# A wider look-ahead window in the build-time plan of TensorE's work

## The chip, the cores and the metric

The kernel runs on one core of a Trainium2 chip. The metric is the device time of one execution in microseconds, taken as the median of several runs. TensorE (PE) multiplies matrices, VectorE (DVE), ScalarE (ACT) and GpSimd (POOL) do the elementwise work, and SyncE (SP) issues most DMAs. Each engine works through its own queue in order; between engines, semaphores order the work. Matrix products land in eight PSUM banks of 512 fp32 columns.

## The reference

One transformer block on 2048 tokens of width 1024, in bf16:

```
h   = x + attention(layernorm(x))
out = h + ((relu(n W_gate) * (n W_up)) W_down),   n = layernorm(h),  W_gate, W_up: 1024 x 3584

attention(n):
  q, k, v = split(n W_qkv) into 32 heads of 32
  pq, pk  = phi(q), phi(k)          # phi(t) = (t + 1 if t > 0 else exp(t)) + 1e-6
  kv, z   = pk^T v, sum over tokens of pk
  o       = (pq kv) / (pq z + 1e-6)
  return o W_o
```

## The kernel before

All large products are done by a seven-product form of the 2 x 2 block matrix product (Strassen-Winograd). A `Quad` holds one such block: its methods `p1` to `p7` issue the seven products, each into a PSUM bank; `fork` copies a bank to a second bank and `snap` copies one to SBUF, both on ScalarE; `out` holds what is done with a finished quarter. Products 1, 6 and 7 add onto one bank (A), 5 and 3 onto another (E); product 2 adds onto the copy of A, product 4 onto A itself. `Quads.run` interleaves quads: products 4 and 3 of a quad are issued after product 1 of the next. Sums and differences of the operand blocks are made beforehand by VectorE.

The stages, in order of time: the first layernorm with K and V (to about 120 us), Q and the attention output (about 120 to 220 us), gate and up (220 to 569 us), and down, where each of the seven products is itself a seven-product block (`deep`, 569 us to the end).

The stage around the first part of the change is the second. Each of the 16 token tiles (`Tile_`) has numerator products (`group` 0, 1 and 2: three, three and two matmuls of 132 columns), divided by the denominators on ScalarE and VectorE into `o`; a transposing DMA into `oT`; and the output projection `wo` in two halves of eight 512-column matmuls. `group` and `wo` take turns with PSUM banks 5, 6 and 7. VectorE adds the input to each half of `wo` and so empties its bank; from this come `h`, its normalisation (one pass on ScalarE, one on POOL), a second transposing DMA, and the operand sums `left_sums`. The function `steps` lays out numerators of tile m beside `wo` of tile m - 2. Into this list the quads of Q for the second half of the tokens (`q_quad(1, c, ...)`) put their products of four matmuls.

In the gate and up stage, `load_group` loads weight columns, `GW.sums` makes their differences on VectorE, `wd_sums` loads a row of W_down, makes four differences and stores them to DRAM (`r_dram`), and `spill` stores sums of the activations (`s_dram`, `l_dram`).

None of this is issued as it is written. From line 568 to the end of `block_kernel`, `nc` is a `Plan`, which records every call as a node with what it must wait for; consecutive matmuls onto one bank that form one accumulation are one node. `Plan.issue` then sorts all nodes by a model of the machine (`cost`, `schedule`) and issues them in that order, with each engine's order fixed. Every instruction therefore has line 123 in the profile.

For TensorE, each node has a nominal time `nom`: the sum of the durations of the matmuls written before it. When TensorE is free, `schedule` takes, of the nodes that are ready, the one with the lowest `nom`, but it looks only at nodes within `WINDOW` nanoseconds of the oldest node that is not yet placed:

```
limit = nodes[pe[first]].nom + self.WINDOW
a = [i for i in a if nodes[i].nom <= limit]
```

The other engines go by `late`, the latest time at which a node may start. Nodes on one engine are taken to follow each other with no delay (`r = clock[e] if w.eng == e else end`), two DMAs on SP too.

Of the kernel before, what the change touches and what calls it, by code (L numbers as in the profile page):

```python
# [32 lines left out]
class Plan:  # L33
# [3 lines left out]

    G = 64
    SEM = 100.0
    WINDOW = 6000.0  # L40
    AHEAD = 120000.0
    OPENING = 45000.0
    MIXED = (120000.0, 215000.0)
# [159 lines left out]
    def schedule(self):  # L203
# [14 lines left out]
        while True:  # L218
            best = None
            for e in engines:  # L220
# [8 lines left out]
                if e == "tensor":  # L229
                    while first < len(pe) and pe[first] in done:  # L230
                        first += 1
                    limit = nodes[pe[first]].nom + self.WINDOW
                    a = [i for i in a if nodes[i].nom <= limit]
# [1340 lines left out]
```

## Time and profile before

| | us |
|---|---|
| median of 7 runs | 724.74 (724.42 to 725.39) |
| profiled execution | 725.2 |
| its span | 723.4 |
| TensorE busy | 711.4 (98%) |
| VectorE busy | 568.9 (79%) |
| ScalarE busy | 278.0 (38%) |
| POOL busy | 56.5 (8%) |

The span is the time from the first to the last instruction of the profiled execution; 1.8 us lie around it. Times in the text are microseconds from the start of the span. The trace is of one execution, the median that of seven runs, and the two differ by 0.5 us. "PE" in a row is a matmul, "PEld" a weight load; a name before the arrow is written, one after it read (`mem` is the one SBUF tile, `psum` the PSUM tile, `tiny` the small one). In the list of waits, a row has the waiting engine, what it waited for, and total, count and longest wait.

### The profile page before, as it was taken

The numbers are of one execution on the slowest core, as the hardware profiler recorded it, in microseconds if no ns is written. First come the engines' busy times: TensorE is split into PE (matmuls) and PEld (weight loads), VectorE is DVE, ScalarE is ACT, GpSimd is POOL, SyncE is SP. The second block draws the span as 40 slices with busy tenths as digits, with TensorE's granted clock in tenths as the row PEclk, the third lists the DMA queues.
The fourth block names the chain that finished last, engine by engine and source line by source line (L and its number), as shares of the span: only waits on it lengthen the run. The fifth ranks groups of instructions, "written<-read, shape, count | busy, mean of one in ns | idle before, by whom it ended". The sixth has DMA issues, their size and how long they took to land.

```text
span 723.4 us, 11146 instructions
## 1 busy us (share of the span) xinstructions
PE 711.4 (98%) x4112; PEld 396.8 (55%) x4163; DVE 568.9 (79%) x966; ACT 278.0 (38%) x548; POOL 56.5 (8%) x62
## 2 busy tenths in 40 slices
PE   8899999999999999999999999999999999999998
PEld 4444445444444444444444444444444688888887
DVE  6899665788797975666766968769768879899996
ACT  5787655665655343333333333333333220001100
POOL 0000000002101120000000000000000004001452
PEclk9999999999999999999999999999999999999999
DMA  9556506159955540446245584685591878777974
GB/s 290 147 97 134 163 1 200 35 109 199 213 107 146 137 96 8 134 129 189 64 138 178 170 258 132 205 261 182 165 299 57 277 266 206 217 263 241 244 76 60
DMA packets 156503, 117.40 MB, mean 162 GB/s; under 512 B 54944, under 2 KB 140192, under 8 KB 156320
## 3 DMA queue, kind: packets, MB, share of 16 engines
q1 hardware_dynamic: 148832, 113.01, 53.8%
q0 software_dynamic: 7616, 3.67, 4.8%
q8 instruction: 32, 0.52, 0.3%
q14 instruction: 23, 0.19, 0.1%
HBM read 70.52 MB, written 34.08 MB: 145 GB/s over the span
## 4 chain that ended last, share of the span: by engine, by line
PE 87%; DVE 6%; DMA 3%; ACT 3%; issue 1%; SPq 0%; DVEq 0%; ACTq 0%
PE psum L123 87%; DVE mem L123 5%; ACT mem L123 2%; DMA mem<-mem 2%; DMA mem<-in_A_wqkv_dram 1%; DVE tiny L123 1%; ACT tiny L123 1%; SPq L123 0%; ACT psum L123 0%; DVEq L123 0%; ACTq L123 0%
## 5 line engine op out<-in xcount | busy, mean ns | idle before, releaser
L123 PE MATMUL psum<-mem 128*128 128x512 bf16 (+4 forms) x4096 | 710.6, 334 | 8.6 <-DVE mem L123 2.6
L123 PEld LDWEIGHTS <-mem 128*128 128x128 f16 (+1 forms) x4163 | 396.8, 98 | 322.9 <-issue 9.5
L123 DVE TENSOR_TENSOR mem<-psum,mem 128x512 f32<-128x512 f32 (+2 forms) x240 | 187.2, 793 | 97.4 <-ACT mem L123 64.7
L123 DVE TENSOR_TENSOR mem<-mem 128x512 f16<-128x512 bf16 (+8 forms) x400 | 241.1, 643 | 9.7 <-DMA mem<-mem 3.7
L123 ACT COPY mem<-psum 128x512 f32<-128x512 f32 (+2 forms) x124 | 92.6, 749 | 212.4 <-PE psum L123 206.2
L123 ACT COPY psum<-psum 128x512 f32<-128x512 f32 (+1 forms) x68 | 49.1, 722 | 157.9 <-PE psum L123 157.9
L123 POOL DMA_DIRECT2D out_dram<-mem x28 | 34.1, 1300 | 412.1 <-DVE mem L123 412.0
L123 ACT ACTIVATE mem<-psum 128x512 bf16<-128x512 f32 x90 | 53.5, 597 | 19.8 <-PE psum L123 19.2
L123 DVE SCALAR_TENSOR_TENSOR mem<-mem 128x512 bf16<-128x512 bf16 (+1 forms) x71 | 57.6, 812 | 1.2
L123 DVE SCALAR_TENSOR_TENSOR mem<-psum,mem 128x512 bf16<-128x512 f32 x66 | 45.4, 689 | 14.8 <-PE psum L123 12.5
L123 POOL TENSOR_SCALAR mem<-mem,tiny 128x1024 bf16<-128x1024 bf16 x16 | 20.7, 1296 | 244.2 <-ACT tiny L123 244.2
L123 ACT ACTIVATE mem<-mem,tiny 128x1024 bf16<-128x1024 bf16 x24 | 27.5, 1145 | 5.2 <-DVE tiny L123 5.0
L123 DVE TENSOR_SCALAR mem<-mem 128x512 bf16<-128x512 bf16 (+1 forms) x49 | 16.5, 339 | 15.4 <-ACT mem L123 15.1
L123 ACT ACTIVATE tiny<-tiny 128x1 f32<-128x1 f32 (+2 forms) x120 | 23.9, 205 | 7.4 <-DVE tiny L123 4.5
L123 ACT ACTIVATE mem<-mem 128x1024 bf16<-128x1024 f32 (+1 forms) x23 | 24.3, 1056 | 5.1 <-DVE mem L123 3.1
L123 DVE TENSOR_TENSOR mem<-psum,tiny 128x384 bf16<-128x384 f32 (+1 forms) x48 | 22.8, 507 | 4.0 <-ACT tiny L123 3.5
L123 ACT ACTIVATE tiny<-psum 128x12 f32<-128x12 f32 (+1 forms) x48 | 8.0, 170 | 18.5 <-PE psum L123 17.8
L123 DVE BATCH_NORM_STATS2 tiny<-mem 128x6 f32<-128x512 bf16 x16 | 10.3, 680 | 2.3 <-DMA mem<-in_A_x_dram 2.3
L123 ACT CAST mem<-psum 128x512 bf16<-128x512 f32 x18 | 10.3, 581 | 3.3 <-PE psum L123 2.9
L123 DVE TENSOR_SCALAR mem<-mem,tiny 128x1024 bf16<-128x1024 bf16 x16 | 8.6, 540 | 3.7 <-ACT tiny L123 3.6
L123 ACT ACTIVATION_READ_ACCUMULATOR mem<-mem,tiny 128x1 f32 x24 | 4.5, 188 | 0.0
L123 DVE TENSOR_SCALAR tiny<-tiny 128x1 f32<-128x1 f32 x16 | 3.4, 210 | 0.4
(17 smaller groups left out, 12.2 us busy)
## 6 DMA issues: line engine op xcount, KB each, us to landing
l_dram<-mem SPq DMA_DIRECT2D x98, 128.0 KB, 2.3
mem<-l_dram SPq DMA_DIRECT2D x12, 896.0 KB, 6.2
mem<-in_A_x_dram SPq DMA_DIRECT2D x32, 256.0 KB, 3.1
mem<-in_B_W_up_dram SPq DMA_DIRECT2D x14, 512.0 KB, 5.6
mem<-in_B_W_gate_dram SPq DMA_DIRECT2D x14, 512.0 KB, 4.5
mem<-in_B_W_down_dram SPq DMA_DIRECT2D x28, 256.0 KB, 3.5
r_dram<-mem SPq DMA_DIRECT2D x56, 128.0 KB, 2.4
mem<-r_dram SPq DMA_DIRECT2D x8, 896.0 KB, 5.1
```

The costliest lines, as they stand in the source:

```text
L123: call = lambda: getattr(getattr(self.nc, eng), op)(*args, **k)
```

## The change

One constant of the planner changes. The window within which it may pull a TensorE node ahead of older ones grows from 6000 to 10000 ns of nominal matmul time. The number of instructions, their sizes and the memory layout stay; the order on TensorE, VectorE, ScalarE and SP is planned anew.

```
 class Plan:
     G = 64
     SEM = 100.0
-    WINDOW = 6000.0
+    WINDOW = 10000.0
     AHEAD = 120000.0
     OPENING = 45000.0
     MIXED = (120000.0, 215000.0)
...
                 if e == "tensor":
                     while first < len(pe) and pe[first] in done:
                         first += 1
                     limit = nodes[pe[first]].nom + self.WINDOW
                     a = [i for i in a if nodes[i].nom <= limit]
                     if not a:
                         continue
```

More of the change, by code (lines that the diff above doesn't have):

```diff
@@ L39 @@
     SEM = 100.0
-    WINDOW = 6000.0
+    WINDOW = 10000.0
     AHEAD = 120000.0
```

## The prediction

> **What bounds the kernel now.** First the busy shares, then TensorE's clock, then the chain that ended last.
>
> ```profile
> PE 711.4 (98%) x4112; PEld 396.8 (55%) x4163; DVE 568.9 (79%) x966; ACT 278.0 (38%) x548; POOL 56.5 (8%) x62
> ...
> PEclk9999999999999999999999999999999999999999
> ...
> PE 87%; DVE 6%; DMA 3%; ACT 3%; issue 1%; SPq 0%; DVEq 0%; ACTq 0%
> ```
>
> TensorE is busy 98% of the span at the full granted clock and carries 87% of the chain. The change adds or removes no instruction, so it can only fill TensorE's idle time or make more of it. How much is there? Ends of matmuls are modelled, so I use starts: in a full stretch a 512-column matmul starts every 0.2158 us, and 4163 weight loads against 4112 matmul records mean that 51 records are missing; a gap of exactly one matmul is a missing record unless the weight loads (none is missing) show it too. What remains after 140 us is short:
>
> ```
> at us    idle   what TensorE went on with
> 148.66   0.14   numerator products
> 150.76   0.89   output projection (wo) of tile 0
> 165.34   0.21   wo, tile 3, first half
> 170.63   0.51   wo, tile 4, first half
> 175.92   0.51   wo, tile 5, first half
> 193.46   0.16   product 3 of a Q quad
> 206.75   0.39   product 6 of a gate/up quad
> 268.58   0.20   product 3 of a gate/up quad
> 573.81   0.10   product 6 of a down quad
> ```
>
> Together 3.1 us, 0.43% of the time: that is all that this change can win. Nothing stands between 270 and 570 us, nor after 574. TensorE's waits between 148 and 270 us and the stages say the same:
>
> ```profile
> PE psum L123 <- DMA mem<-mem: 0.7, 1, 0.7
> PE psum L123 <- DVE mem L123: 0.7, 2, 0.3
> PE psum L123 <- ACT psum L123: 0.2, 1, 0.2
> ...
> 154.69:182.94 28.25, 27.35 (x151) 13.31 (x151) 22.50 (x54) 17.37 (x59) 6.38 (x6) 1.00 0.90 192
> ...
> 217.30:568.86 351.56, 349.94 (x1625) 160.34 (x1653) 260.12 (x462) 125.99 (x201) 11.19 (x8) 1.00 0.53 157
> ```
>
> The columns of the stage rows are stretch, length, busy PE, PEld, DVE, ACT and POOL, clock, DMA share, GB/s. The chain shows what is behind the largest gaps:
>
> ```profile
> 147.51 3.20 DMA mem<-mem
> 150.71 0.05 issue
> 150.76 2.88 PE psum L123 x14
> ...
> 163.53 0.77 DVE mem L123
> 164.30 0.30 issue
> 164.60 0.18 DVE mem L123
> 164.78 0.43 issue
> 165.21 0.09 DVE mem L123
> 165.29 0.04 issue
> 165.34 1.01 PE psum L123 x4
> ```
>
> The first is the transposing DMA that turns tile 0's attention output for wo. The second is a PSUM bank: the next wo needs the bank of the wo before it, which VectorE empties only after a 1.15 us subtraction that stands ahead in its queue:
>
> ```profile
> 163.53 1.15 DVE L123 TENSOR_TENSOR mem<-mem 128x1024 f16<-128x1024 bf16 x1
> 164.60 0.68 DVE L123 SCALAR_TENSOR_TENSOR mem<-psum,mem 128x512 bf16<-128x512 f32 x1
> ```
>
> The gaps at 170.63 and 175.92 have the same pair ahead of them (1.15 us from 168.81 and from 174.10).
>
> **The change, part by part.** A wider WINDOW lets the planner take a TensorE group whose nominal place lies up to 10 us behind the oldest unplaced group instead of 6 us. Comparing the two instruction orders, TensorE's is the same up to about 150 us; 104 of its 957 groups change places, at 150-183, 192-202, 206-211 and 571-587 us of the present trace. VectorE, ScalarE and SP are reordered there, and VectorE and SP also at about 390-550 us. POOL keeps its order.
>
> *150-183 us.* In steps of six numerator matmuls, one product, wo, two numerators, wo, the products shift by one:
>
> ```
> filler ahead of wo of tile   0    1    2    3    4        5        between wo 6 and wo 7
> before                       -    p6   p5   p7   p2       p1 next  p4
> after                        p6   p5   p7   p2   p1 next  p4       -
> ```
>
> The gap at 150.76 is thus filled. Product 6 has four matmuls, 4 x 0.2158 = 0.863 us; it adds onto a bank whose copy (ScalarE, 148.51 to 149.09) is done, so it runs 149.87 to 150.73 and wo 0 starts at 150.76 as before. The gain comes 32 us later, where no product stands between wo 6 and wo 7: -0.86.
>
> Here the Trainium skill speaks against the change: "TensorE: Matmul & The Clock Gate", under "Back-to-back issue gap", says that a sustained load-and-multiply stream settles at about 131 ns for a 512-column matmul. Product 6 would then be 0.52 us of work: 0.34 us less to win and 0.36 us of the gap left. This trace has 215.8 ns in every full stretch; I take the trace.
>
> The next stalls change because the evacuations come a step earlier. I follow the queues with this trace's durations: last matmul start to its reader 0.41 us (0.25 for a 132-column one), ScalarE to VectorE 0.04, VectorE to TensorE 0.06.
> - Tile 3 (0.21): the 1.15 us subtraction is no longer ahead of the bank read. VectorE reads at 164.10 (bound by wo itself) to 164.78 and TensorE arrives at 165.13: no stall, -0.21.
> - Tile 4 (0.51): the same; bank read 168.89-169.57, TensorE at 169.91: -0.51.
> - Tile 5 (0.51): one subtraction now does stand ahead, 173.14-174.29, then the read to 174.89. TensorE arrives at 174.70 and starts at 174.95: 0.25 is left, -0.26.
> - Wo of tile 7, late next: TensorE arrives 0.97 us closer to the normalisation that precedes its transposing DMA. VectorE ends that at 178.51, TensorE arrives at 181.97. The eight such transposes between 147 and 180 us land 3.04 to 4.18 us after issue, mean 3.30, the one for this tile 3.56. At 3.56 it lands at 182.10: +0.19, between 0 and +0.8.
>
> *192-202 us.* A numerator matmul moves ahead, 0.06 us of fill in the 0.16 us gap; VectorE gets one subtraction of 0.68 us earlier, into the 0.4 us that it waits for ScalarE. I take -0.05, bounds -0.16 to +0.3.
>
> *206-211 us.* Product 6 waits for ScalarE's bank copy (0.57 us); now product 5, whose bank is free, goes first: -0.39. Two numerators then come 0.86 us sooner against a VectorE read, by the same following +0.14.
>
> *571-587 us.* Products of the first two down quads are interleaved otherwise; the copy that product 6 waits for again has one 0.76 us group beside it: 0, bounds -0.1 to +0.8 (one such group uncovered).
>
> *390-550 us, VectorE and SP.* W_down subtractions (0.42 us each) and their DMAs move. They cost nothing while TensorE's products cover them: 12.1 us of matmuls a quad against about 9 us of VectorE (260.12 of 351.56 busy), with 1.8 us to spare in the banks (the product that reuses a bank comes two products of 1.73 us later; the read takes 0.41 + 1.22 of these). Uncovered, each lateness counts in full. On SP one move sets a wait, see the second rival.
>
> Sum: -0.86 -0.21 -0.51 -0.26 +0.19 -0.05 -0.39 +0.14 = -1.95, say **-1.9 us**. The profiled execution took 725.2 us (span 723.4, 1.8 around it), the median of the seven runs is 724.74; what is around the span does not change. 725.2 becomes 723.3, the median **722.8 us**. A difference of 0.2%, 1.45 us, is about what a measurement of this kernel tells from no change, so the forecast is just past it.
>
> **Rivals.**
> 1. *The gain is given back at once.* The first fill only moves TensorE 0.86 us closer to what is late next, and in steps with wo on both sides VectorE's and ScalarE's latencies set the pace (the chain between 160 and 180 us is 25% DVE and 29% ACT and only 32% PE). If tile 7's transpose takes 4.18 us (+0.8 instead of +0.19) and one bank read is late again (+0.5), -0.85 is left: 723.9, no difference that can be told. For it: transposes are slowest at 174 us, where the DMA engines are busy 90%. Against it: each subtraction that made a bank late has visibly moved.
> 2. *Slower: SP blocks.* At 473.6 us the new order puts the load of a W_down row directly behind the stores that read its buffer. SP issues in order, so it stands until the store has landed:
>
> ```profile
> 471.21 2.44 SPq L123 DMA_DIRECT2D r_dram<-mem  x3
> 474.25 0.38 SPq L123 DMA_DIRECT2D mem<-in_B_W_gate_dram  x1
> 474.68 2.14 SPq L123 DMA_DIRECT2D s_dram<-mem  x2
> 476.91 0.41 SPq L123 DMA_DIRECT2D mem<-in_B_W_up_dram  x1
> ```
>
> That store landed at 477.58, 6.4 us after its issue, behind two 512 KB weight loads. So SP stands 3.9 us, and behind it wait two spills and the last group's second gate and up halves (474.25 and 476.91 now, about 478.6 and 479.0 then). They land by about 484.5; their first reader is a VectorE subtraction at 489.26, about 487.3 when all is 2 us earlier. The W_down subtraction that is pulled ahead of a gate/up read (from 492.1 to about 483.3) has its row at about 481. Margins 2.5 us, plus the 1.8 us of slack in the banks. It decides if these transfers land over 4.3 us later than reckoned, as VectorE then stands ahead of a PSUM read; to end slower by 0.2% it must cost 3.4 us, and over the several such places might cost 4: 724.74 - 1.9 + 4 = 726.8. Against it: SP stood so in the present order too, with no gap in TensorE between 270 and 570 us.
> 3. *It does nothing.* Filling shifts the stall to the next wo and no step gets shorter: 724.7. Against it: the 0.89 us was a single wait for a DMA that the filler does not delay.
>
> **How the numbers follow.** Gain as worked out 0.56; given back 0.28; nothing 0.08; slower 0.08. The first has its own range of -1.5 to -2.4, nearly all past 1.45, and the first rival a few hundredths past it: faster 0.59, within 0.2% 0.33, slower 0.08. The range reaches from -2.7 (nearly all of the 3.1 us) to +0.3 (no gain and one late down group's part): 722.0 to 725.0 us.
>
> **What would show it.** Right: no TensorE gap near 150.8, a p6 of 0.86 us there; wo of tiles 3 and 4 unstalled, a rest of about 0.25 at tile 5; wo of tile 7 starting about 1.6 us earlier; TensorE about 2 us ahead from 212 us to the end. Wrong: gaps at tiles 3 and 4 as before, over 0.8 us at tile 7, or any gap between 270 and 570 us; then SP's waits and the W_down loads are the place to look.

## The result and the profile after

The kernel after the change takes 723.06 us (median of 15 runs, 722.27 to 723.71) beside 724.92 us (median of 35 runs) for the kernel before: ratio 0.9974, 95% interval 0.9968 to 0.9981, which is 1.86 us or 0.26% faster. The forecast was 722.8 us in a range of 722.0 to 725.0, with 0.59 on faster. The profiled execution took 722.55 us, its span is 720.8 us.

The page of the kernel after, busy shares, TensorE's clock and the chain that ended last:

```profile
PE 710.9 (99%) x4112; PEld 396.4 (55%) x4163; DVE 568.8 (79%) x966; ACT 278.5 (39%) x548; POOL 56.7 (8%) x62
...
PEclk9999999999999999999999999999999999999999
...
PE 90%; DVE 5%; DMA 2%; ACT 2%; issue 1%; SPq 0%; DVEq 0%; ACTq 0%
```

TensorE's work and clock are the same; only its share of the chain grew, from 87% to 90%. Three short stretches of the chain show where:

```profile
145.79 6.33 PE psum L123 x40
...
160.77 8.45 PE psum L123 x46
...
173.35 0.13 DVE mem L123
173.48 0.48 issue
173.96 0.09 DVE mem L123
174.04 0.04 issue
174.09 4.38 PE psum L123 x21
178.47 0.05 issue
178.52 3.62 PE psum L123 x16
```

The columns are start, length and what. In the first stretch TensorE runs through from 145.79 to 152.12, past the place where it had waited 0.89 us for tile 0's transposing DMA. In the second it runs from 160.77 to 169.22, past wo of tiles 3 and 4, where it had waited for VectorE's bank reads (those of tile 3 had been in the chain from 163.53). At tile 5 VectorE's read is still in the chain, and TensorE starts at 174.09. VectorE's rows at tile 3 and at tile 5:

```profile
163.25 0.69 DVE L123 SCALAR_TENSOR_TENSOR mem<-psum,mem 128x512 bf16<-128x512 f32 x1 [0.51 <-PE psum L123]
...
172.27 1.15 DVE L123 TENSOR_TENSOR mem<-mem 128x1024 f16<-128x1024 bf16 x1
173.35 0.68 DVE L123 SCALAR_TENSOR_TENSOR mem<-psum,mem 128x512 bf16<-128x512 f32 x1
```

At tile 3 the bank read now waits 0.51 us for wo itself; the 1.15 us subtraction no longer stands ahead of it. At tile 5 it still does, as it did at all three tiles in the kernel before.

The stretches between corresponding places of TensorE's order, after (columns as in the stage rows of the prediction):

```profile
147.75:153.83 6.08, 6.03 (x39) 3.08 (x38) 5.24 (x13) 2.94 (x10) 0.00 (x0) 1.00 0.46 88
153.83:181.11 27.28, 27.02 (x150) 13.32 (x151) 22.79 (x56) 17.31 (x58) 5.96 (x5) 1.00 0.94 199
181.11:214.63 33.52, 33.26 (x174) 15.90 (x176) 31.08 (x64) 19.69 (x53) 3.62 (x3) 1.00 0.70 160
214.63:566.20 351.57, 349.94 (x1624) 160.28 (x1653) 259.22 (x460) 125.99 (x201) 11.31 (x8) 1.00 0.53 157
```

and those of the kernel before, of which the prediction showed the second and the last:

```profile
148.66:154.69 6.03, 5.25 (x34) 2.76 (x34) 5.24 (x13) 2.35 (x9) 0.00 (x0) 1.00 0.47 88
...
183.80:217.30 33.50, 33.11 (x174) 16.00 (x176) 30.16 (x63) 19.93 (x52) 2.39 (x2) 1.00 0.68 153
```

The first stretch, up to the filler ahead of wo of tile 1, holds four more matmuls (38 weight loads beside 34; the matmul records, 39 and 34, are not complete) and is only 0.05 us longer: the fill. The second, up to wo of tile 7, went from 28.25 to 27.28 us: the bank reads. Product 4, 0.86 us between wo 6 and wo 7 in the kernel before (182.94 to 183.80), is no longer there. The third (33.50 and 33.52) and the last (351.56 and 351.57) did not move. Together 0.05 - 0.97 - 0.86 + 0.02 = -1.76 us.

The two spans differ by more, 2.6 us. The first of these places comes at 148.66 in one profile and at 147.75 in the other, and up to there the orders are the same. So those 0.91 us are no effect of the change. To compare profiles without it, I use one stretch from here on: from the first numerator weight load after product 4 of the output stage (at 148.31 before, 147.39 after) to the weight load of the gate/up product 3 (268.17 and 265.49). It measures 119.86 us before and 118.10 after. From its end to TensorE's last weight load it is 451.38 us in both.

### The profile page after: what moved, and what is told of

Its sections match the earlier page's. It is cut to its first block, busy times and chain, and to the rows that moved or that the text cites. A ratio compares the mean times of both kernels' runs of the same rounds, so it can differ in the third digit from the quotient of the medians.

```text
span 720.8 us, 11146 instructions
## 1 busy us (share of the span) xinstructions
PE 710.9 (99%) x4112; PEld 396.4 (55%) x4163; DVE 568.8 (79%) x966; ACT 278.5 (39%) x548; POOL 56.7 (8%) x62
## 4 chain that ended last, share of the span: by engine, by line
PE 90%; DVE 5%; DMA 2%; ACT 2%; issue 1%; SPq 0%; DVEq 0%; ACTq 0%
PE psum L123 90%; DVE mem L123 4%; ACT mem L123 1%; DMA mem<-mem 1%; DMA mem<-in_A_wqkv_dram 1%; DVE tiny L123 1%; ACT tiny L123 0%; SPq L123 0%; ACT psum L123 0%; DVEq L123 0%; ACTq L123 0%
```

## The experiments

The first six change one line of the kernel before, in `schedule`:

```
-                    limit = nodes[pe[first]].nom + self.WINDOW
+                    t = nodes[pe[first]].nom
+                    limit = t + (...)
```

Only what stands in the brackets is given below, in nanoseconds. The last ones change a constant, in the kernel after or before, or nothing. Each ratio is to the kernel before on the chip of that run, where its median was 724.68 to 725.07 us. My theory: the gain comes from product 6 ahead of tile 0's wo and from the VectorE queue that shifts with it, up to tile 7. Rivals: each bit of window brings its share (A); the gain is made after 270 us or by other reorderings (B); the fill alone is the gain (C).

| run | median us | ratio to before (95%) | stretch us | end of it to the last weight load |
|---|---|---|---|---|
| before | 724.74 | | 119.86 | 451.38 |
| after | 723.06 | 0.9974 (0.9968 to 0.9981) | 118.10 | 451.38 |
| 8.5 us | 724.63 | 0.9996 (0.9987 to 1.0005) | 119.90 | 451.38 |
| 8.8 us | 723.18 | 0.9971 (0.9959 to 0.9982) | 118.18 | 451.38 |
| only at 140-180 | 723.13 | 0.9972 (0.9961 to 0.9984) | 117.97 | 451.38 |
| all but 140-180 | 724.81 | 0.9995 (0.9986 to 1.0004) | 119.68 | 451.38 |
| fill alone | 725.25 | 1.0004 (0.9995 to 1.0013) | 119.60 | 451.37 |
| 25 us | 723.92 | 0.9990 (0.9981 to 0.9998) | 119.11 | 451.37 |
| after, again | 722.56 | 0.9968 (0.9956 to 0.9981) | 117.96 | 451.37 |
| waiting rule to 260 | 722.32 | 0.9971 (0.9960 to 0.9981) | 118.15 | 451.37 |
| waiting rule 20-600 | 721.50 | 0.9952 (0.9938 to 0.9966) | 117.90 | 451.17 |
| waiting rule 20-215 | 722.23 | 0.9963 (0.9950 to 0.9975) | 117.91 | 451.38 |
| waiting rule 20-600, window 6 us | 723.86 | 0.9986 (0.9977 to 0.9995) | 119.90 | 451.18 |

**A window of 8.5 and of 8.8 us.** `8500.0` and `8800.0`.

> Window of 8.5 us. The planner still cannot reach product 6 from the oldest node when TensorE waits for tile 0's transpose, but products of the first two down quads (571-586 us) and some VectorE and SP work are already reordered. Theory (the gain is the fill ahead of tile 0's wo and what follows from it at 150-183 us): the 0.89 us gap at 150.8 and the gaps at tiles 3, 4 and 5 stay, and the time is that of the kernel before within 0.3 us (about 724.9). Rival A (each us of window gives its share): 2.5 of the 4 us, so about -1.2 us, 723.7. Rival B (the gain comes from the reordering after 270 us): about -1.8 us, 723.1.

> Window of 8.8 us: product 6 is now just within reach ahead of tile 0's wo. TensorE's order is that of the window of 10 us at 150-185, 206-213 and 571-586 us, without the reordering at 192-202. Theory: the whole gain is there at once, -1.7 to -1.9 us (about 723.1), with no gap over 0.1 at 150.8 and none at tiles 3 and 4. Rival A (by share of the window): -1.3 us, 723.6, and hardly different from the window of 8.5 us. Rival B (the reordering after 270 us): the same as the window of 8.5 us.

The stretch goes from 119.86 to 119.90 with 8.5 us and to 118.18 with 8.8 us: a step, not a slope. Product 6 lies 8.66 us of nominal time behind the oldest unplaced node at that moment; a window that reaches it has the gain, one that does not has none. With 8.5 us TensorE's list of waits at 140-270 us is as before:

```profile
PE psum L123 <- DMA mem<-mem: 0.8, 1, 0.8
PE psum L123 <- DVE mem L123: 0.7, 2, 0.3
PE psum L123 <- ACT psum L123: 0.2, 1, 0.2
```

(This list is made from modelled ends and leaves out the shorter stalls, such as the 0.21 us of tile 3.) Of the change's order this kernel has TensorE's at 571-586 us and SP's from 586 us on, and it is no faster. Rival A falls, and B for that part.

**The wide window only at 140-180 us of nominal time, and everywhere else only.** `10000.0 if 140000.0 < t < 180000.0 else 6000.0`, and the two numbers exchanged.

> 10 us of window only where the oldest unplaced node has its nominal place between 140 and 180 us, 6 us elsewhere: the change's order at 150-185 and 206-213 us alone. Theory: -1.6 to -1.8 us (about 723.2), since the stalls at 150.8, tiles 3 to 5, tile 7 and 206 are all here and nothing else had a gap to lose. Rival B: 0, 724.9.

> The complement: 6 us of window at nominal 140-180 us, 10 us elsewhere; the change's order at 192-209 and 571-586 us and its VectorE and SP order after 270 us, without the fill. Theory: 0 to -0.3 us (724.6 to 724.9), with the gaps at 150.8 and at tiles 3, 4 and 5 as before. Rival B: -1.5 us or more (723.4). If zone and this one add up to the whole change, the two parts do not interact.

The first has the whole gain (the stretch 117.97), the second 0.18 us of it in the stretch and nothing that its times can tell. TensorE's waits at 140-270 us in the first:

```profile
PE psum L123 <- ACT psum L123: 0.2, 1, 0.2
```

and in the second:

```profile
PE psum L123 <- DMA mem<-mem: 0.8, 1, 0.8
PE psum L123 <- DVE mem L123: 0.7, 2, 0.3
```

The DMA and VectorE waits are what the first took away; the ScalarE wait (product 6 of the gate/up quad for its bank copy) is what the second took away. With the first, as with 8.8 us, product 6 still stands ahead of product 5 there and waits 0.38 us: the expectations were wrong to count the change's order at 206-213 us to these two kernels. With the second that wait is gone, but two numerators behind it wait 0.22 us for VectorE at 208.86.

Rival B falls for the places that the second kernel reorders. What it does not test is VectorE and SP at 270-570 us: its records there stand in the order of the kernel before, contrary to its expectation. For that part there are two other measurements: the time from 266 us to the end is 451.38 us before and after, and the next kernel, which has most of the change's order at 410-550 us, gains nothing. On top of the first part the second adds nothing: the whole change has 118.10 and, in its second run, 117.96. It takes 0.19 us at 206 and brings a wait of 0.23 us at 214.5 (below).

**The fill alone.** `10000.0 if 146000.0 < t < 147000.0 else 6000.0`: product 6 goes ahead of tile 0's wo, and TensorE's other products stay where they were. VectorE and SP change too, but not before 410 us: at 410-550 us their order is, but for a few places, that of the change.

> 10 us of window only where the oldest unplaced node has its nominal place at 146 to 147 us: product 6 goes into the gap ahead of tile 0's wo, product 5 then stays where it was ahead of wo of tile 2, so the step of tile 1 has no product, and from there all is as before the change. Theory (the fill is only a loan; it counts because every following product moves a step ahead too and leaves the missing product to a place where nothing is late): the gap at 150.8 goes (-0.8), wo of tile 1, with no filler ahead of it, waits about 0.65 us for VectorE to empty its bank, tiles 3, 4 and 5 stall as before: about -0.2 us, 724.7. Rival C (the fill by itself is the gain): -0.8 us, 724.1.

725.25 us, no gain, and the time from 266 us to the end is 451.37 us, so the reordering at 410-550 us brings none either; the stretch is 0.26 us shorter where -0.2 was reckoned. The chain at the next step:

```profile
149.87 3.64 PE psum L123 x18
153.51 0.03 issue
153.53 0.71 DVE mem L123 x2
154.24 0.04 issue
154.29 1.89 PE psum L123 x8
```

The 0.9 us wait at 149.9 is gone, and tile 1's wo, with no product ahead of it, waits 0.60 us for VectorE to empty its bank; the stalls of tiles 3, 4 and 5 (0.21, 0.51 and 0.51) stand as before. Rival C falls. A filler taken from a later step only moves the hole there. It pays when the whole row of fillers moves up, and the hole ends at a step where nothing is late: between wo 6 and wo 7. VectorE's order at 160-195 us is planned anew together with the row; no run changes one of the two without the other, so their shares are not told apart.

**A window of 25 us.** `25000.0`.

> Window of 25 us: the planner pulls products ahead from still further off, at 130-209 us. Following the queues with the durations of the trace after the change: the products run out two steps sooner, tiles 4 and 5 wait 0.06 and 0.26 us, and at about 205 us the numerators with nothing to run beside them wait 0.9 us; about -0.8 us against the kernel before, 724.1, or 0.5 to 1.0 us longer than with the window of 10 us. Rival A (further is better): as with 10 us or below, 723.0 or less.

The stretch is 119.11, 1.0 us longer than with 10 us and 0.75 shorter than before. Tiles 4 and 5 wait 0.26 and 0.51 us, more than I reckoned (0.06 and 0.26): VectorE's 1.15 us subtraction stands ahead of the bank read at both again (from 168.57 and 173.86). At 204.4 us the numerators wait 0.78 (0.9 reckoned):

```profile
201.92 1.87 PE psum L123 x13
203.79 0.56 DVE mem L123
204.35 0.04 issue
204.39 1.62 PE psum L123 x8
```

Product 1 of a gate/up quad is issued directly ahead of these numerators; before the change, and with 10 us, product 4 of the quad before it stands between. Here product 4 comes only behind them and product 5. So the wait is not one for want of products, as I had reckoned it: product 4 (0.86 us) would cover 0.78 us, but stands behind the wait. The total came out near the -0.8 us that I expected, of parts that differ. Why the plan came out so was not looked into.

**The change again, and the rule by which VectorE and ScalarE wait.** `schedule` lets these engines hold a long operation back for one that is due over 1.5 us sooner and becomes ready within 1.2 times its length; outside `MIXED` the factor is 0.5. With the window of 10 us, in three kernels (to 260, 20-600 and 20-215):

```
-    MIXED = (120000.0, 215000.0)
+    MIXED = (120000.0, 260000.0)
```

```
-    MIXED = (120000.0, 215000.0)
+    MIXED = (20000.0, 600000.0)
```

```
-    MIXED = (120000.0, 215000.0)
+    MIXED = (20000.0, 215000.0)
```

The second of these was also run with the window of 6 us, and the change itself once more.

> The kernel after the change, with the rule by which VectorE and ScalarE may wait for work that is due sooner extended from 215 to 260 us (TensorE's order is unchanged): meant for the 0.23 us that the third numerator group waits at 214.5 us. Expected: that gap goes, -0.25 us against the window of 10 us, about 722.8 where that gives 723.05; if the wait is not VectorE's order but its load, no difference.

> As the one before, with the rule in force from 20 to 600 us: also for the layernorm stage (a wait of TensorE of 0.8 to 1.5 us at 30 us for a VectorE result) and for gate and up (0.2 us at 266 us). Expected: 0.5 us from the opening, 0.2 at 266 and 0.25 at 214: about -1.0 us against the window of 10 us, 722.0. If the opening's wait is set by the DMAs instead, only -0.45, 722.6; if idle VectorE time in gate and up makes a W_down row late, slower than 723.1.

> The change as it is, on the chip of the next two runs: about 723.0, and the stretch from the numerators of the first output step to product 3 at 266 us again 1.7 to 1.8 us shorter than before. Tile 7's projection waits between 0 and 0.4 us, according to how long its transposing DMA takes (0 at 3.2 us, 0.4 at 3.57).

> The kernel after the change with the waiting rule of VectorE and ScalarE in force from 20 instead of 120 us, to 215 us as now. Expected: the part of the gain of the run from 20 to 600 us that comes from the layernorm stage, -0.5 to -0.8 us against the change alone (722.4), with the same stalls after 140 us as the change. If that run's gain came from after 215 us, 723.0.

> The rule from 20 to 600 us with the old window of 6 us. If the two edits add up: about -1.4 us against the kernel before (723.4), the stalls at 150.8 and at tiles 3 to 5 as before, none at 30 us above 0.5. If they work on the same stalls, the time is that of both together, 721.5.

The change again: 722.56 us, and the stretch, 117.96, is 1.90 us shorter than before where 1.7 to 1.8 was expected. Tile 7's wo does not wait.

To 260: the wait at 214.5 is gone, TensorE runs through there:

```profile
212.97 5.21 PE psum L123 x30
```

but in this run tile 7's transpose was slower (next section; 0.17 us) and the wait at 192 us longer (0.25 instead of 0.15), and the stretch is 118.15, as after. Whether it is faster than the change its times do not tell.

20-600: 721.50 us, 3.2 us below the kernel before on its chip and the fastest version here. It gained in the opening and after 210 us. The wait at 30 us fell to 0.45 us, and those of 0.3 and 0.5 at 69 and 83 us are gone, with new ones of 0.60 at 55.5 and 0.22 at 67.9. The wait of 0.23 at 214.5 us is gone, and so is that of 0.20 at 266, which lies just behind the weight load that ends the stretch (451.17 instead of 451.38 to the end). The page:

```profile
PE 713.4 (99%) x4163; PEld 396.6 (55%) x4163; DVE 568.1 (79%) x966; ACT 278.4 (39%) x548; POOL 56.0 (8%) x62
...
PE 94%; DVE 2%; ACT 2%; DMA 1%; issue 0%; ACTq 0%
```

PE's share of the chain is 94%. It was not run on one chip with the change alone, and the interval of the second run of the change (0.9956 to 0.9981) overlaps its own, so how much it adds to the change is less sure than that both beat the kernel before.

20-215: the numerators come at 146.43, earlier than in any profile of the old opening (147.28 to 148.36), and the stalls after 140 us are the change's; the time, 722.23 beside 722.56 for the change on the same chip, cannot be told from it.

With the window of 6 us the rule has -1.2 us where -1.4 was expected. The stalls at 150.4 and at tiles 3 to 5 (0.93, 0.22, 0.51, 0.51) are back, and the wait at 30 us is 0.76 where under 0.5 was expected. The two edits work on different stalls, and the times agree with that: 0.9986 times 0.9968 is 0.9954, beside 0.9952 for both together, each to about 0.001.

## Why the prediction was right

Step by step, as gaps in matmul starts:

| step of the prediction | said | measured |
|---|---|---|
| product 6 ahead of wo of tile 0 | -0.86 | -0.81 (0.08 of the 0.89 is left) |
| tile 3 | -0.21 | -0.21 |
| tile 4 | -0.51 | -0.51 |
| tile 5 | -0.26 (0.25 left) | -0.25 (0.26 left) |
| wo of tile 7 | +0.19 (0 to +0.8) | 0 in this profile, 0.17 and 0.19 in two others |
| 192-202 us | -0.05 | -0.02 (-0.16 in the second run; see below) |
| 206 us, product 5 for product 6 | -0.39 | -0.19 |
| two numerators against a VectorE read | +0.14 | 0 |
| not named: the third numerator group at 214.5 us | | +0.23 |
| 571-587 us | 0 | 0 |
| 390-550 us, VectorE and SP | 0 | 0 |
| sum | -1.95 | -1.76 |

- The fill. Product 6's matmuls start 0.216 us apart (149.17, 149.39, 149.60), so it covers 0.86 us, as the prediction took it from the trace. The 0.52 us were an estimate from the sustained 131 ns that the Trainium skill states in "TensorE: Matmul & The Clock Gate", "Back-to-back issue gap"; the measured 216 ns decides. The transposing DMA landed at 149.85, and wo started at 149.90.
- The step of tile 7 is there, and its size depends on the run. Tile 7's transpose took 3.19 to 3.20 us from issue to landing in four profiles with this order (after twice, only at 140-180, 20-215), 3.37 with 8.8 us and 3.56 and 3.57 in the other two. With 3.2 TensorE does not wait; with 3.37 the weight load waits 0.19 but its matmul does not yet; at 3.56 the matmul starts 0.17 late (182.25 instead of 182.07, both with the rule to 260), near the 0.19 that the prediction gave for 3.56. The term was priced with the latency of a single profile, and in the profile of the change it is 0.
- The wait at 192 us is not set by this edit. With the old order of TensorE there it is 0.16 (before, 8.5 us), 0.23 (8.8 us) or nothing (only at 140-180); with the new one 0.15 (after), nothing (after, again) or 0.25 (to 260).
- At 206 us the step failed in part. Product 5 went first and product 6 no longer waited, but product 3, which now comes directly behind product 5, waits 0.20 us at 204.72, for the second of two VectorE operand differences, which ends at 204.66:

```profile
203.91 0.75 DVE L123 TENSOR_TENSOR mem<-mem 128x512 f16<-128x512 bf16 x2
```

  Before, product 3 came one product (product 6, 0.86 us) and one wait (0.39) later and met them done. The prediction asked of the group that was moved what it waits for, and not of the one that came next.
- The wait at 214.5 us was missed. Bank 7, which this numerator group reuses, is emptied by VectorE from 213.77, behind a 0.69 us difference:

```profile
213.16 0.69 DVE L123 TENSOR_TENSOR mem<-mem 128x1024 f16<-128x1024 bf16 x1
213.77 0.69 DVE L123 SCALAR_TENSOR_TENSOR mem<-psum,mem 128x512 bf16<-128x512 f32 x1
```

  The prediction ended its following of the queues at 211 us and named no reader after it. The wait stands in both profiles of the change and with 20-215, and is gone when the waiting rule reaches it. Together these misses make the stretch from wo 7 to 214.6 us worth nothing (33.50 and 33.52), where the prediction had -0.30 from 192 us on. The run with the wide window at 140-180 alone, with product 6's wait of 0.39 still there and none at 214.5, has the same total.
- The second rival named the right place, and what it feared there cost nothing, as the prediction had reckoned. SP stood at the W_down load behind the stores; its waits at 466-486 us:

```profile
SPq L123 <- DMA r_dram<-mem: 5.0, 2, 3.6
SPq L123 <- DVE mem L123: 2.2, 4, 1.1
SPq L123 <- DMA mem<-in_B_W_up_dram: 0.4, 1, 0.4
```

  and what it issued after it stood:

```profile
468.56 2.31 SPq L123 DMA_DIRECT2D r_dram<-mem  x3
474.56 0.33 SPq L123 DMA_DIRECT2D mem<-in_B_W_down_dram  x1
474.95 0.90 SPq L123 DMA_DIRECT2D s_dram<-mem  x2
475.94 0.43 SPq L123 DMA_DIRECT2D mem<-in_B_W_gate_dram  x1
```

  3.6 us where 3.9 were reckoned. TensorE's chain there shows the usual pieces of 12.03 us for one quad, and from 266 us to the end all profiles in which the waiting rule ends by 260 us agree within 0.01 us. What those transfers would cost with less cover was not tried. The prediction also has SP reordered at 150-211 us; by the traces its order first differs at 384 us. No term of the sum rests on that.
- The first rival, given back at once, did not come: no bank read that had been freed was late again.
- The time itself: -1.9 was said, 1.86 is the difference of the medians and 1.76 that of the stretch. The interval of the ratio leaves room for 1.4 to 2.3 us, so that 1.86 lies so near to 1.9 is in part luck. The forecast named -0.21, -0.51, -0.26 and the fill, and these make the gain; the smaller terms summed to -0.11, and to about 0 on the chip, where the misses at tile 7, at 206 and at 214.5 us partly set each other off.

## What to carry to other kernels

A filler pulled forward is a loan: follow it to the step that it left, and count the gain only where the hole ends beside nothing that is late. Look-ahead in a list scheduler can act in a step, at the distance of the node that fits: here nothing at 8.5 us and the whole gain at 8.8. More is not better by itself: 25 us gave back 1.0 of the 1.8 us. When profiles of two versions differ at a place ahead of the first reordered instruction, that part is not the change: compare a stretch between the same two instructions.

## What was unexpected in the hardware

The opening differs from run to run with the same order. The first numerator weight load of the compared stretch comes between 147.28 and 148.36 us in nine profiles whose order up to there is the same. All of it is made before 69 us, by the start itself (one product's weight load comes at 27.75 to 28.81) and by the wait at 30 us behind it (0.76 to 1.5 us); after 266 us the same profiles agree within 0.01 us. The latency of one and the same transposing DMA (tile 7's) ranged from 3.19 to 3.57 us over the seven profiles in which its neighbours on the queue were the same. And the matmul records were 51 short in the first profiles of before and after only; the eleven others have all 4163, so a count of idle time that rests on matmul records alone can mislead from one run to the next, while the weight loads were complete in every one.
